# Fewer plain units, more seven-product pairs, and one h matmul moved, in the last stage of a fused retention, soft-MoE and MLP kernel

## The chip, the cores and the metric

The kernel runs on one core of one Trainium2 chip. The metric is device microseconds (us) per execution. The engines are PE (TensorE, with its weight loads as PEld), DVE (VectorE), ACT (ScalarE), POOL (GpSimd) and SP (SyncE, which only issues DMAs here). Each engine works through its own list of instructions in the order written.

## The reference

Three parts follow each other on 3072 tokens (4 batches of 768) of 512 features, all in float32:

```python
# 1 retention: per batch and head, a decayed running state
state = gamma * state + k[t] (x) v[t];  y[t] = scale * q[t] @ state
# 2 soft mixture of experts: 8 experts with 4 slots each
logits = x @ phi                        # 3072 x 32
slot_input = softmax(logits, tokens).T @ x
slot_out = relu(slot_input @ w1[e]) @ w2[e]
x = softmax(logits, slots) @ slot_out
# 3 MLP
h = x @ w_in                            # 3072 x 2048
g = h * sigmoid(1.702 * h)
out = g @ w_out                         # 3072 x 512
```

## The kernel before, in words

The change lies in part 3. There h has a short form: x is a mix of 32 slots, so h = c @ (slot_out @ w_in). The kernel forms G = slot_out @ w_in once (`make_g1`, `make_g2`, tiles `gp`, `rp`, `gst`), and one matmul with 512 columns then gives h of 128 features for 512 tokens. The cost is in g @ w_out.

The tokens stand in six blocks of 512 (block 0 to 5), the 2048 features in sixteen columns f of 128, or eight pairs r of two. To keep float32 precision with a fast matmul type, each operand is split in a high and a low part, and a product is three matmuls (high·high, high·low, low·high). A pair r of one block is done in one of two ways:

- As two plain units. A unit is one h matmul (L641), two ACT activations (L643, L645), the low part on DVE (`lo_unit`, L651, tile `gl`), and twelve matmuls of 512 columns into four banks `acc` (L664): 13 matmuls.
- As one seven-product unit, here called a pair unit. It multiplies 2x2 blocks by a scheme with seven products in place of eight: 7 products x 2 x 3 = 42 matmuls of 256 columns (L727, tiles `P1` to `P7`), and two h matmuls (`s_h`, L693, bank `hb`). For it DVE and ACT build sums of g (`forms`), their high parts `ha`, `hs` (L711) and low parts `la`, `ls`.

`NPL` says how many columns of each block are plain; they come first, in one loop (L1141), block 1 to 5, then the rest of block 0. Its pass u, "step u" from here on, issues h of unit u, the low part of unit u-1, a portion of other work, and the twelve matmuls of unit u-2. The portion is what `work(BUD)` takes from a queue: it runs items until their costs (set by hand, `C1`, `C2` and others) have used up BUD. The queue holds the preparation of the weights: for j = 1, 2, 3 the narrowing of w_in from 64-bit words (`win`, L164 to L168, six DVE instructions for each of two halves), the narrowing of one pair r of w_out (`wfa` or `wfb`, six more), its sums, the G matmuls (`gp`, then `Gh`, `Gl`, then `rp`), and the split of the pair in `bh`, `bl` (L623 on ACT, L688 on DVE). After the loop's units come passes NU and NU+1 (L1146 to L1161), which also prepare the first pair units.

Then all pair units run, block by block (`s_unit`). At the last pair unit of a block, DVE adds the seven products into the block's result; four of these additions (`finish_block`) are put off. The last `NEND` columns of block 5 are plain again (`end_units`): DVE first runs what was put off, then PE's twelve matmuls of each follow, and after the last column DVE adds six pieces to the result (`put`), each sent out by a DMA.

Of the kernel before, what the change touches and what calls it, by code (L numbers as in the profile page):

```python
# [33 lines left out]
NW = 14  # L34
NQ = 3
NX = 5
NPL = (4, 4, 4, 6, 6, 6)
NEND = 4
FULL = (2, 6, 7)
Q = 256  # L40
NWU = 3
# [1 line left out]
KTP = (0, 1, 2, 3, 8, 13, 16, 20)  # L43
KA = (1, 256, 1, 512)
KW = (2, 1, 2)
BUD = 2.3
C1, C2 = 0.34, 0.6
WL = (3, 2)

# [2 lines left out]
def retention_soft_moe_mlp(  # L52
# [575 lines left out]
    def plain_w(f):  # L628
        if f in wh:
            return wh[f], wl[f]  # L630
        return [x[f // 2][:, 2 * (f % 2):2 * (f % 2) + 2].rearrange("p s d -> p (s d)") for x in (bh, bl)]

    units = [(0, f, 0, 1) for f in range(2)]
    units += [(b, f, 0, NPL[b] - 1) for b in range(1, NB) for f in range(NPL[b])]
    units += [(0, f, 2, NPL[0] - 1) for f in range(2, NPL[0])]
    NU = len(units)

    def h_unit(u):
        b, f = units[u][0:2]
        hp = pf.tile([P, 512], F32, tag="h", name=f"h{u}", bufs=3)  # L640
        mm(hp, lhsT=gst[:, f * P:(f + 1) * P], rhs=cT[:, 512 * b:512 * b + 512], start=True, stop=True)  # L641
        gh = fp.tile([P, 512], F32R, tag=("ha", "hs")[u % 2], name=f"gh{u}", bufs=2)
        nc.scalar.activation(out=gh, in_=hp, func=AF.Gelu_apprx_sigmoid)  # L643
        gg = FT[0][:, 2 * (u % 4):2 * (u % 4) + 2].rearrange("p s d -> p (s d)")
        nc.scalar.activation(out=gg, in_=hp, func=AF.Gelu_apprx_sigmoid)  # L645
        gl = fp.tile([P, 512], F32R, tag=("la", "ls")[u % 2], name=f"gl{u}", bufs=2)
        g_hl[u] = (gg, gh, gl)

    def lo_unit(u):
        gg, gh, gl = g_hl[u]  # L650
        nc.vector.tensor_tensor(out=gl, in0=gg, in1=gh.bitcast(F32), op=ALU.subtract)  # L651

    def o_unit(u, t0=0, t1=4, terms=(0, 1, 2)):
        b, f, f0, f1 = units[u]
        _, gh, gl = g_hl[u]
        w0, w1_ = plain_w(f)
        ops = [(gh, w0), (gh, w1_), (gl, w0)]
        if f == f0 and 0 in terms:
            for t in range(t0, t1):
                acc[t] = pf.tile([P, DM], F32, tag="acc", name=f"acc{u}_{t}", bufs=5)  # L660

        def term(t, n):
            g, w = ops[n]
            mm(acc[t], lhsT=g[:, t * P:(t + 1) * P], rhs=w, start=f == f0 and n == 0, stop=f == f1 and n == 2)  # L664

        if u == 0:
            for n in terms:
                for t in range(t0, t1):
                    term(t, n)
        for t in range(t0, t1):  # L670
            if u > 0:
                for n in terms:
                    term(t, n)
            if f == f1 and f0 == 0:
                nc.scalar.copy(out=stage[:, t], in_=acc[t])
                nc.sync.dma_start(out=parts[b][:, t], in_=stage[:, t])
            elif f == f1:
                nc.vector.tensor_tensor(out=pt[0][:, t], in0=acc[t], in1=pt[0][:, t], op=ALU.add)

    span_ = [(NPL[b] // 2, 8 - NEND // 2 * (b == NB - 1)) for b in range(NB)]  # L680
    pairs = [(b, r) for b in range(NB) for r in range(*span_[b])]
# [5 lines left out]
    def vadd(out_, a, b_, op=ALU.add):  # L687
        nc.vector.tensor_tensor(out=out_, in0=a, in1=b_, op=op)  # L688

    def s_h(n, a):  # L690
        b, r = pairs[n]
        f = 2 * r + a
        mm(PB["h"], lhsT=gst[:, f * P:(f + 1) * P], rhs=cT[:, 512 * b:512 * b + 512], start=True, stop=True)  # L693
        t = FT[0]
        nc.scalar.activation(out=t[:, 3 * a:3 * a + 2].rearrange("p s d -> p (s d)"), in_=PB["h"],  # L695
                             func=AF.Gelu_apprx_sigmoid)
        if a == 0:
            vadd(t[:, 2], t[:, 0], t[:, 1], ALU.subtract)

    def s_sum1():  # L700
        t = FT[0]
        vadd(t[:, 5:7], t[:, 0:4:2], t[:, 3:4].to_broadcast([P, 2, Q]))

    def s_sum2():
        t = FT[0]
        vadd(t[:, 7], t[:, 4], t[:, 6], ALU.subtract)

    def s_hi(n, k):
        c0, c1 = FORM[k]
        AH[n, k] = fp.tile([P, c1 - c0, Q], F32R, tag="h" + k, name=f"h{k}_{n}", bufs=2)  # L710
        nc.scalar.copy(out=AH[n, k], in_=FT[0][:, c0:c1])  # L711

    def s_lo(n, k):
        c0, c1 = FORM[k]
        AL[n, k] = fp.tile([P, c1 - c0, Q], F32R, tag="l" + k, name=f"l{k}_{n}", bufs=2)
        vadd(AL[n, k], FT[0][:, c0:c1], AH[n, k].bitcast(F32), ALU.subtract)
# [83 lines left out]
    def end_h(x):  # L800
        f, b = KFF - NEND + x, NB - 1
        mm(PB["h"], lhsT=gst[:, f * P:(f + 1) * P], rhs=cT[:, 512 * b:512 * b + 512], start=True, stop=True)
        gh = fp.tile([P, 512], F32R, tag=("ha", "hs")[x % 2], name=f"egh{x}", bufs=2)
        nc.scalar.activation(out=gh, in_=PB["h"], func=AF.Gelu_apprx_sigmoid)
        gg = FT[0][:, 2 * x:2 * x + 2].rearrange("p s d -> p (s d)")
        nc.scalar.activation(out=gg, in_=PB["h"], func=AF.Gelu_apprx_sigmoid)
        gl = fp.tile([P, 512], F32R, tag=("la", "ls")[x % 2], name=f"egl{x}", bufs=2)
        end_hl[x] = (gg, gh, gl)
# [5 lines left out]
    def end_units():  # L814
# [11 lines left out]

        for x in range(NEND):
            f = KFF - NEND + x
            w0, w1_ = plain_w(f)
            _, gh, gl = end_hl[x]  # L830
            ops = [(gh, w0), (gh, w1_), (gl, w0)]
            last = x == NEND - 1
            if last:
                put(3, slice(0, DM), at_[3], False)
            for t in range(3 if last else 4):
                for i, (g, w) in enumerate(ops):
                    mm(at_[t], lhsT=g[:, t * P:(t + 1) * P], rhs=w, start=x == 0 and i == 0,  # L837
                       stop=i == 2 and (last or (t == 3 and x == NEND - 2)), skip_group_check=True)
                if t == 1 and x + 2 < NEND:
# [11 lines left out]
    with tc.manual_schedule():  # L851
# [241 lines left out]
        def work(budget):  # L1093
            while budget > 0:
                if not queue and not ready:
                    if todo:
                        todo.pop()()
                    elif pend:
                        ready.append(pend.pop(0)[1])
                    else:  # L1100
                        return
                c, fn = (ready or queue).pop(0)
                fn()
                budget -= c
                for p in pend:
                    p[0] -= c
                ready.extend(p[1] for p in pend if p[0] <= 0)
                pend[:] = [p for p in pend if p[0] > 0]
# [32 lines left out]
        for u in range(5, NU + 2):  # L1141
            if u < NU:
                h_unit(u)
                lo_unit(u - 1)
                work(BUD)
            elif u == NU:  # L1146
                lo_unit(u - 1)
                work(1000)
                assert len(raws) == 1 and not (queue or todo or pend or ready), raws
                PB["h"] = pf.tile([P, 512], F32, tag="h", name="hb", bufs=3)  # L1150
                s_h(0, 0)
            else:
                s_h(0, 1)
                s_sum1()
                s_hi(0, "a")
                s_sum2()
                s_lo(0, "a")
                s_hi(0, "s")
                s_lo(0, "s")
                s_h(1, 0)  # L1160
            o_unit(u - 2)  # L1161
        for p, tag in ((2, "acc"), (4, "h"), (1, "h"), (7, "acc"), (5, "acc"), (6, "acc"), (3, "acc")):
            PB[p] = pf.tile([P, 2, Q], F32, tag=tag, name=f"P{p}", bufs=3 if tag == "h" else 5)
        n7 = [x for p_ in zip(pair_narrow(7, 0), pair_narrow(7, 1)) for x in p_]
# [83 lines left out]
```

## Time and profile before

| | |
|---|---|
| median of 3 runs | 453.2 us (453.13 to 453.81) |
| the profiled execution: time, span | 453.41 us, 451.6 us |
| PE, DVE, ACT busy | 97%, 74%, 45% |
| PE clock granted | full speed (2.4 GHz) in all slices |

The span is what the profiler's records cover; 1.8 us of the execution's time lie outside. The retention and expert parts fill the first 160 us, the plain units run from there to 264 us, the pair units to 436 us, the end units and the last DMAs to the end. PE is nearly always busy, so the questions are how much PE work a change removes and whether PE then has to wait.

### The profile page before, as it was taken

Reading aid. Unit: us, or ns where it says so; the run is one execution under the profiler, and the core shown is the slowest. Engines: PE = TensorE matmul, PEld = TensorE weight load, DVE = VectorE, ACT = ScalarE, POOL = GpSimd, SP = SyncE. Lnnn points to the kernel's source line nnn. Section 1 sums busy time; section 2 is a strip of 40 time slices with the busy share of each in tenths; the row PEclk is TensorE's granted clock in tenths of the full one; section 3 lists DMA queues with packets and bytes.
Section 4 is the critical chain, followed back from the end, with each engine's and each line's share of the span. In section 5 each row is a group of like instructions: output and inputs, shape, how many; then the busy total and the mean of one; then the engine's idle time right before and its main releaser. Section 6 shows DMA issues by size and latency. Waiting matters only on the chain.

```text
span 451.6 us, 9953 instructions
## 1 busy us (share of the span) xinstructions
PE 436.6 (97%) x4125; PEld 362.9 (80%) x4125; DVE 332.7 (74%) x594; ACT 205.2 (45%) x351; POOL 48.3 (11%) x53
## 2 busy tenths in 40 slices
PE   8999999899999989999999999999999999999996
PEld 4877877687433467788888889999999999999995
DVE  2455665565455577988979789897797797988984
ACT  1323232323120166563657655655555565565530
POOL 3344343434000000000000000000000000000000
PEclk9999999999999999999999999999999999999999
DMA  8999999998899958588455402001301301311022
GB/s 297 407 401 402 402 371 406 339 405 315 315 394 409 382 211 280 162 304 286 155 218 187 161 26 94 1 1 46 112 30 48 138 4 48 140 46 50 20 75 93
DMA packets 27693, 92.40 MB, mean 205 GB/s; under 512 B 2880, under 2 KB 4320, under 8 KB 23296
## 3 DMA queue, kind: packets, MB, share of 16 engines
q1 hardware_dynamic: 27248, 91.24, 54.8%
q8 instruction: 32, 0.52, 0.5%
q10 hardware_dynamic: 288, 0.36, 0.3%
q0 software_dynamic: 112, 0.16, 0.1%
q14 instruction: 13, 0.11, 0.1%
HBM read 79.17 MB, written 12.58 MB: 203 GB/s over the span
## 4 chain that ended last, share of the span: by engine, by line
PE 83%; DMA 10%; DVE 3%; ACT 1%; issue 1%; POOL 0%; DVEq 0%; SPq 0%; ACTq 0%; POOLq 0%
PE P L727 34%; PE acc L664 18%; DMA qt<-qt_dram 10%; PE sc L212 4%; PE hb L693 4%; PE hp L487 3%; PE y L261 3%; PE eo L512 3%; PE y L257 2%; PE P L837 2%; PE h L641 1%; PE xp L282 1%; PE wu L867 1%; PE op L368 1%; PE tq L530 1%; PE st L269 1%
## 5 line engine op out<-in xcount | busy, mean ns | idle before, releaser
L688 DVE TENSOR_TENSOR forms<-forms 128x256 f32<-128x256 f32 (+1 forms) x93 | 47.5, 511 | 22.4 <-ACT forms L695 21.0
L695 ACT ACTIVATE forms<-hb 128x512 f32<-128x512 f32 x62 | 37.1, 598 | 54.7 <-PE hb L693 34.9
L664 PE MATMUL acc<-wo_hl,gh 128*128 128x512 f32 x192 | 59.8, 394 | 0.4 <-ACT gh L643 0.4
L727 PE MATMUL P<-bh,la 128*128 128x256 f32 x208 | 58.9, 283 | 0.0
L727 PE MATMUL P<-bl,ha 128*128 128x256 f32 x208 | 58.8, 283 | 0.0
L727 PE MATMUL P<-bh,ha 128*128 128x256 f32 x208 | 58.7, 282 | 0.0
L216 DVE TENSOR_TENSOR pt<-sc,ca_t 128x512 f32<-128x512 f32 x44 | 28.3, 685 | 22.9 <-PE sc L212 22.9
L727 PE MATMUL P<-bh,hs 128*128 128x256 f32 x156 | 44.1, 283 | 0.0
L727 PE MATMUL P<-bh,ls 128*128 128x256 f32 x156 | 44.1, 282 | 0.0
L727 PE MATMUL P<-bl,hs 128*128 128x256 f32 x156 | 44.0, 282 | 0.0
L664 PEld LDWEIGHTS acc<-wo_hl,gh 128*128 128x128 f32 x192 | 35.4, 188 | 8.1 <-issue 0.6
L727 PEld LDWEIGHTS P<-bl,ha 128*128 128x128 f32 x208 | 39.4, 189 | 1.1
L727 PEld LDWEIGHTS P<-bh,ha 128*128 128x128 f32 x208 | 39.4, 190 | 0.0
L727 PEld LDWEIGHTS P<-bh,la 128*128 128x128 f32 x208 | 39.4, 189 | 0.0
L688 DVE TENSOR_TENSOR la<-forms,ha 128x1024 fp32r<-128x1024 f32 x31 | 37.9, 1222 | 0.0
L664 PE MATMUL acc<-wo_hl,gl 128*128 128x512 f32 x96 | 37.3, 394 | 0.3 <-DVE gl L651 0.3
L711 ACT CAST ha<-forms 128x1024 fp32r<-128x1024 f32 x31 | 32.6, 1051 | 6.4 <-DVE forms L688 5.6
L643 ACT ACTIVATE gh<-h 128x512 fp32r<-128x512 f32 x30 | 18.0, 600 | 32.7 <-PE h L641 23.9
L711 ACT CAST hs<-forms 128x768 fp32r<-128x768 f32 x31 | 26.0, 838 | 10.1 <-DVE forms L688 7.4
L727 PEld LDWEIGHTS P<-bl,hs 128*128 128x128 f32 x156 | 29.5, 189 | 1.2
L727 PEld LDWEIGHTS P<-bh,hs 128*128 128x128 f32 x156 | 29.5, 189 | 0.0
L727 PEld LDWEIGHTS P<-bh,ls 128*128 128x128 f32 x156 | 29.5, 189 | 0.0
(224 smaller groups left out, 915.3 us busy)
## 6 DMA issues: line engine op xcount, KB each, us to landing
w<-w_dram SPq DMA_DIRECT2D x36, 512.0 KB, 7.7
w<-w_dram SPq DMA_DIRECT2D x14, 1024.0 KB, 8.7
ktv<-ktv_dram SPq DMA_DIRECT2D x20, 512.0 KB, 8.3
wi<-w_in_dram SPq DMA_DIRECT2D x7, 1024.0 KB, 5.6
wo<-w_out_dram SPq DMA_DIRECT2D x7, 1024.0 KB, 4.9
parts<-stage SPq DMA_DIRECT2D x24, 256.0 KB, 3.4
pt<-parts SPq DMA_DIRECT2D x6, 1024.0 KB, 4.8
qt<-qt_dram SPq DMA_DIRECT2D x21, 256.0 KB, 6.4
```

What stands on the lines that cost most here:

```text
L212: mm(sc[hh][:, a, :], lhsT=kT[hh * D:(hh + 1) * D, a, :], rhs=q_[hh * D:(hh + 1) * D, a, :], start=True, stop=True)
L216: nc.vector.tensor_tensor(out=pt[hh], in0=sc[hh], in1=mask[:, None, :].to_broadcast([P, NP, P]), op=ALU.mult)
L261: mm(out_(a, hh ^ (a & 1)), lhsT=vt[:, 2 * a + (hh ^ (a & 1)), :], rhs=pt[hh ^ (a & 1)][:, a, :], start=(c == 0 and a < 2), stop=True, ski ...
L487: mm(hp[32 * j:32 * j + 32, :], lhsT=slotT[:, k, :], rhs=w[:, j, :], start=(k == 0), stop=(k == KDM - 1))
L512: mm(op[32 * j:32 * j + 32, :], lhsT=hT[:, kk, 32 * j:32 * j + 32], rhs=w[:, j, :], start=(kk == 0), stop=(kk == 3))
L643: nc.scalar.activation(out=gh, in_=hp, func=AF.Gelu_apprx_sigmoid)
L664: mm(acc[t], lhsT=g[:, t * P:(t + 1) * P], rhs=w, start=f == f0 and n == 0, stop=f == f1 and n == 2)
L688: nc.vector.tensor_tensor(out=out_, in0=a, in1=b_, op=op)
L693: mm(PB["h"], lhsT=gst[:, f * P:(f + 1) * P], rhs=cT[:, 512 * b:512 * b + 512], start=True, stop=True)
L695: nc.scalar.activation(out=t[:, 3 * a:3 * a + 2].rearrange("p s d -> p (s d)"), in_=PB["h"], func=AF.Gelu_apprx_sigmoid)
L711: nc.scalar.copy(out=AH[n, k], in_=FT[0][:, c0:c1])
L727: mm(PB[p][:, t], lhsT=g[:, c], rhs=w, start=r == span_[b][0] and t == 0 and i == 0, stop=r == span_[b][1] - 1 and i == 2, skip_group_chec ...
```

## The change

```diff
-NPL = (4, 4, 4, 6, 6, 6)
-NEND = 4
+NPL = (4, 4, 4, 4, 6, 6)
+NEND = 2
...
-BUD = 2.3
+BUD = 2.5
...
                 s_lo(0, "a")
                 s_hi(0, "s")
                 s_lo(0, "s")
-                s_h(1, 0)
             o_unit(u - 2)
+        s_h(1, 0)
```

Block 3 has four plain columns in place of six, and block 5 two in place of four at the end. So the loop has 28 units (NU) where it had 30, there are 33 pair units where there were 31, and two end units where there were four. The 25 steps that call `work(BUD)` become 23, and each may take 2.5. The first h of the second pair unit, `s_h(1, 0)`, is issued behind the last plain unit's twelve matmuls, not ahead of them.

In the loop the new budget changes what stands between two low parts on DVE. Of DVE's list, from step 7 on; `gl6` is the low part of unit 6, `win1` and `wfa` are the weights being prepared, `Gl512` is the low part of G that the second group of G matmuls needs. Before:

```order
L651 TENSOR_TENSOR gl6_2461<-forms_2266,gh6_2458 128x512
L168 SCALAR_TENSOR_TENSOR win1_2438<-wi1_1_2363,win1_2438 128x512 x2
L164 TENSOR_SCALAR wfa_2135<-wo2_2436 128x512 x2
L166 SCALAR_TENSOR_TENSOR wfa_2135<-wo2_2436,wfa_2135 128x512
L651 TENSOR_TENSOR gl7_2487<-forms_2266,gh7_2484 128x512
L166 SCALAR_TENSOR_TENSOR wfa_2135<-wo2_2436,wfa_2135 128x512
L168 SCALAR_TENSOR_TENSOR wfa_2135<-wo2_2436,wfa_2135 128x512 x2
L688 TENSOR_TENSOR wfa_2135<-wfa_2135 128x512
L688 TENSOR_TENSOR wfa_2135<-wfa_2135 128x256 x2
L651 TENSOR_TENSOR gl8_2521<-forms_2266,gh8_2518 128x512
L565 TENSOR_TENSOR Gl512_2573<-gp1_2554,Gh512_2571 128x128
```

And now, from step 6 on:

```order
L651 TENSOR_TENSOR gl5_2434<-forms_2266,gh5_2431 128x512
L164 TENSOR_SCALAR win1_2438<-wi1_1_2363 128x512 x2
L166 SCALAR_TENSOR_TENSOR win1_2438<-wi1_1_2363,win1_2438 128x512 x2
L168 SCALAR_TENSOR_TENSOR win1_2438<-wi1_1_2363,win1_2438 128x512 x2
L651 TENSOR_TENSOR gl6_2462<-forms_2266,gh6_2459 128x512
L164 TENSOR_SCALAR wfa_2135<-wo2_2436 128x512 x2
L166 SCALAR_TENSOR_TENSOR wfa_2135<-wo2_2436,wfa_2135 128x512 x2
L168 SCALAR_TENSOR_TENSOR wfa_2135<-wo2_2436,wfa_2135 128x512 x2
L651 TENSOR_TENSOR gl7_2489<-forms_2266,gh7_2486 128x512
L688 TENSOR_TENSOR wfa_2135<-wfa_2135 128x512
L688 TENSOR_TENSOR wfa_2135<-wfa_2135 128x256 x2
L565 TENSOR_TENSOR Gl512_2550<-gp1_2531,Gh512_2548 128x128
```

Six narrowing instructions stand between two low parts where there were five, so `gl7` is the last low part ahead of `Gl512`, where it was `gl8`.

On PE the same shift moves the second group of G matmuls, `rp1`, of which the second needs `Gl512`. `acc6` are the banks of block 2. Before:

```order
L664 MATMUL acc6_3_2534<-wo_hl1_2134,gh8_2518 128x512 x2
L664 MATMUL acc6_3_2534<-wo_hl1_2134,gl8_2521 128x512
L641 MATMUL h11_2610<-cT_2126,gst_2127 128x512
L572 MATMUL rp1_2617<-Gh512_2571,selhl_2128 128x128
L573 MATMUL rp1_2617<-Gl512_2573,selhl_2128 128x128
```

Now:

```order
L664 MATMUL acc6_3_2555<-wo_hl0_2133,gh6_2459 128x512 x2
L664 MATMUL acc6_3_2555<-wo_hl0_2133,gl6_2462 128x512
L641 MATMUL h9_2568<-cT_2126,gst_2127 128x512
L572 MATMUL rp1_2579<-Gh512_2548,selhl_2128 128x128
L573 MATMUL rp1_2579<-Gl512_2550,selhl_2128 128x128
```

`rp1` stands in step 9, one step behind `gp1`, where it stood in step 11, two steps behind `gp1` in step 9. The second and third round of preparation (j = 2, 3) take five steps each, where they took six.

At the program's end DVE's list loses the low parts of the third and fourth end unit (`egl2`, `egl3`); `pt5` is the result of block 5, `wfa` holds sums of products. Before:

```order
L688 TENSOR_TENSOR pt5_4563<-P5_3245,pt5_4563 128x2x256
L688 TENSOR_TENSOR pt5_4563<-P3_3247,pt5_4563 128x2x256
L688 TENSOR_TENSOR pt5_4563<-pt5_4563,wfa_2135 128x2x256 x4
L688 TENSOR_TENSOR egl2_5122<-forms_2266,egh2_5119 128x512
L688 TENSOR_TENSOR egl3_5140<-forms_2266,egh3_5137 128x512
L688 TENSOR_TENSOR pt5_4563<-P7_3244,pt5_4563 128x512
L688 TENSOR_TENSOR pt5_4563<-P2_3241,pt5_4563 128x512
```

Now:

```order
L688 TENSOR_TENSOR pt5_4525<-P5_3207,pt5_4525 128x2x256
L688 TENSOR_TENSOR pt5_4525<-P3_3209,pt5_4525 128x2x256
L688 TENSOR_TENSOR pt5_4525<-pt5_4525,wfa_2135 128x2x256 x4
L688 TENSOR_TENSOR pt5_4525<-P7_3206,pt5_4525 128x512
L688 TENSOR_TENSOR pt5_4525<-P2_3203,pt5_4525 128x512
L688 TENSOR_TENSOR pt5_4525<-P4_3204,pt5_4525 128x512
```

The six closing additions follow directly on the four that were put off.

## Rows read from the trace of the kernel before

**Rows 1.** The page, busy time and share of the span by engine.

```profile
PE 436.6 (97%) x4125; PEld 362.9 (80%) x4125; DVE 332.7 (74%) x594; ACT 205.2 (45%) x351; POOL 48.3 (11%) x53
```

**Rows 2.** Chain that ended last: start, us, what; plain, pair and block-end pieces.

```profile
240.34 2.72 PE acc L664 x12
243.29 2.72 PE acc L664 x12
...
382.04 3.60 PE P L727 x30
387.52 3.60 PE P L727 x30
```

**Rows 3.** DVE's timeline, steps 5 to 10: start, us, instruction, idle before it.

```profile
179.86 0.68 DVE L651 TENSOR_TENSOR gl<-forms,gh 128x512 fp32r<-128x512 f32 x1
180.46 0.76 DVE L164 TENSOR_SCALAR win<-wi 128x512 uint32<-128x512 uint32 x2
181.13 1.29 DVE L166 SCALAR_TENSOR_TENSOR win<-wi,win 128x512 uint32<-128x512 uint32 x2
182.34 0.69 DVE L168 SCALAR_TENSOR_TENSOR win<-wi,win 128x512 uint32<-128x512 uint32 x1
...
191.63 1.61 DVE L688 TENSOR_TENSOR wfa<-wfa 128x512 f32<-128x512 f32 x3
193.16 0.68 DVE L651 TENSOR_TENSOR gl<-forms,gh 128x512 fp32r<-128x512 f32 x1
193.76 0.28 DVE L565 TENSOR_TENSOR Gl<-gp,Gh 128x128 fp32r<-128x128 f32 x1
```

**Rows 4.** PE's timeline, steps 6 to 11.

```profile
179.78 0.39 PE L641 MATMUL h<-cT,gst 128*128 128x512 f32 x1
...
183.04 0.39 PE L641 MATMUL h<-cT,gst 128*128 128x512 f32 x1
...
189.15 0.39 PE L641 MATMUL h<-cT,gst 128*128 128x512 f32 x1
...
193.33 0.39 PE L641 MATMUL h<-cT,gst 128*128 128x512 f32 x1
...
196.32 0.39 PE L641 MATMUL h<-cT,gst 128*128 128x512 f32 x1
...
196.61 0.28 PE L573 MATMUL rp<-Gl,selhl 128*128 128x128 f32 x1
...
200.22 0.39 PE L641 MATMUL h<-cT,gst 128*128 128x512 f32 x1
```

**Rows 5.** Busy time by engine in the loop's steps.

```profile
178.00:258.00 80.00, 80.00 (x443) 64.94 (x442) 70.33 (x125) 49.30 (x92) 0.00 (x0) 1.00 0.63 212
```

**Rows 6.** Timelines in a later round: PE's h, then DVE's split waiting for ACT.

```profile
213.24 0.39 PE L641 MATMUL h<-cT,gst 128*128 128x512 f32 x1
215.29 2.30 DVE L688 TENSOR_TENSOR bl<-wfb,bh 128x512 fp32r<-128x512 f32 x3 [2.56 <-ACT bh L623]
```

**Rows 7.** Timelines from the last plain unit to the fourth pair unit: PE, DVE, PE.

```profile
260.58 0.39 PE L693 MATMUL hb<-cT,gst 128*128 128x512 f32 x1
261.66 0.50 PE L693 MATMUL hb<-cT,gst 128*128 128x512 f32 x1 [0.69 <-ACT forms L695]
...
261.64 1.15 DVE L688 TENSOR_TENSOR forms<-forms 128x512 f32<-128x512 f32 x2 [2.26 <-ACT forms L695]
...
280.09 1.22 DVE L688 TENSOR_TENSOR la<-forms,ha 128x1024 fp32r<-128x1024 f32 x1
...
281.43 0.32 PE L727 MATMUL P<-bh,la 128*128 128x256 f32 x1
```

**Rows 8.** Timelines of the end: PE's first matmul of the end units, then DVE.

```profile
436.03 0.40 PE L837 MATMUL P<-bh,egh 128*128 128x512 f32 x1
...
441.11 1.49 DVE L688 TENSOR_TENSOR egl<-forms,egh 128x512 fp32r<-128x512 f32 x2
444.87 3.39 DVE L688 TENSOR_TENSOR pt<-P,pt 128x512 f32<-128x512 f32 x6 [2.27 <-PE P L837]
```

## The prediction, made before the changed kernel ran

> **What bounds the kernel now.** I read the page first. PE is busy for 97% of the span, DVE for 74% [rows 1], and the granted clock is at its upper level, 2.4 GHz, throughout, so PE's own work is the first suspect. The chain of waits gives its price: a plain unit starts every 2.95 us (243.29 less 240.34), and a pair unit, with its two h matmuls, every 5.48 (387.52 less 382.04) [rows 2]. PE is continuous there. Then I read DVE's and PE's timelines side by side through the loop, where the budget changes. Over 80 us of it DVE is busy for 70.33 [rows 5]; the 9.7 that are left are not spread evenly. From 179.86 until Gl ends at 194.04 DVE has no idle time at all [rows 3]: it runs one list, and PE waits for results far down in it. PE shows this already: step 6 starts at 179.78 and step 7 at 183.04 [rows 4], 3.26 apart, 0.31 more than a plain unit, because the low part that step 6 needs started only at 179.86. Last I read the change to the pair units and the end, where the additions close the chain [rows 7, 8].
>
> **The change part by part.** All sums are made against the profiled execution, 453.41 us, which is 0.2 above the median of the three runs.
>
> *The units.* Four plain units go (4 x 2.95 = 11.80), two pair units come (2 x 5.48 = 10.96) [rows 2]. On PE alone that is -0.84. The number of block ends stays.
>
> *A rule that speaks against it.* The rows give 2.72/12 = 227 ns per matmul of 512 columns and 3.60/30 = 120 ns per one of 256 [rows 2], so halving the columns nearly halves the price. The Trainium skill, TensorE: Matmul & The Clock Gate, section Back-to-back issue gap, gives streams with weight loads 131 ns at 512 columns and 81 at 128, a price that falls far less than the columns; by an estimate of 98 ns at 256 from that page, a pair unit would take 42 x 0.098 + 2 x 0.131 = 4.4 us against 3.4 for two plain units, and this part would be +1.9. By that rule, the trace disagrees (227 and 120 ns), and the trace decides.
>
> *The budget.* DVE's steps in the rows: a low part takes 0.60 to the next start (179.86 to 180.46), a narrowing pair by shift 0.67, a pair by scalar_tensor_tensor 1.21 (181.13 to 182.34) [rows 3]. A step with a low part and six narrowings so takes 0.60 + 0.67 + 1.21 + 1.21 = 3.69 on DVE, against 2.95 on PE. Before, it was five narrowings, 3.08. The changed list has three such steps in a row in each round. Nothing before 179.86 changes on any engine, so I can walk on from there.
>
> Low part 5 starts at 179.86 + 3.69 = 183.55, low part 6 at 187.23, low part 7 at 190.91; the three sums follow it (0.60 + 0.07 for the start, and 1.53 from 191.63 to 193.16 [rows 3]), and Gl runs from 193.11 to 193.39. On PE, step 7 starts at 183.04 as before and waits for low part 5. From step 6 I take that the wait is the low part's start less the step's start plus 0.23 (0.08 there, wait 0.31): 0.74. Step 8 starts at 183.04 + 2.95 + 0.74 = 186.73. It holds gp now, and a step with gp takes 4.18 (189.15 to 193.33) [rows 4], so step 9 starts at 190.91. Its second G matmul, due 0.29 later at 191.20 (196.61 less 196.32 [rows 4]), needs Gl, which ends at 193.39. It waits 2.2. That is 2.95 in the first round; before, steps 7 and 8 together lost 0.22 (189.15 less 183.04 less 2 x 2.945) [rows 4], so it costs 2.7 more. In the kernel before the same matmul came at 196.61, 2.6 after its Gl: two more units had run.
>
> In a later round the split of the pair starts 2.05 after the step's h (213.24 to 215.29), since ACT's casts stand behind that step's activations, and takes 2.22 to the next start [rows 6]; the next low part starts 4.27 after that h, while a step with rp takes 3.90 (196.32 to 200.22) [rows 4]. So DVE enters the next round 0.37 late, and three steps add 0.74 each: 2.59. Gl then ends 2.59 + 2.20 + 0.28 = 5.07 after its step's h, and rp is due 4.18 + 0.29 = 4.47 after it: a wait of 0.6. The second round is spared: the wait of 2.2 in the first lets DVE enter it some 0.8 early. The third pays 0.6. Behind it the last two pairs of weights bring DVE about 2.9 late again at step 24, by the same counting: 0.2 more.
>
> Waits in the loop: 2.7 + 0.6 + 0.2 = +3.5. Its bounds: the first 2.7 rests on a list without gaps and could only be less if those instructions ran shorter, so I keep 2.5 as the low end; the high end is 4.5, if the casts of the fifth pair, which ACT now runs ahead of block 4's four copies, must wait for all of the sums and PE then waits for its banks. I take 3.5. DMAs: each raw load is issued when a buffer is narrowed and is used at least two steps later; SP issues them behind the stores of the same blocks as before, and I cost this at nothing.
>
> *The moved h.* Before, PE issued one h at 260.58 and the next at 261.66, waiting 0.69 for ACT to empty the bank [rows 7]: 1.08 where a matmul of 512 columns takes 0.23, so the move frees 0.85 on PE. What is late next is DVE. From 261.64, when the first sums start, it runs without a gap through three pair units and the narrowing put between them, until the low part that starts at 280.09 and ends at 281.31; PE's matmul that needs it issues at 281.43 and already waits for it (0.32 where its neighbours take 0.28) [rows 7]. That list starts from the same h at 260.58, so at the fourth pair unit the gain is spent. I take 0; the bounds are -0.85 and +0.2, since the additions of the last plain unit now stand ahead of a sum that ACT's cast needs.
>
> *The end.* The first end matmul is at 436.03, and DVE's last six additions end at 444.87 + 3.39 = 448.26, 12.23 later [rows 8]. With two units less, PE would allow 12.23 - 5.89 = 6.34. But DVE must first finish the last pair's additions and the four put off: it is through with them at 441.11, 5.08 after the first end matmul [rows 8], and that list hangs on the last products, not on the end units, whose two 2.95 us covered it. Six additions of 0.60 or less (two are half as long: 3.2 in all) then end at 8.3. So 1.9 of the 5.89 is given back; bounds 1.7 and 2.1, by the row's 3.39.
>
> Sum: -0.84 + 3.5 + 0 + 1.9 = +4.6. The profiled execution would take 458.0, a median 457.8.
>
> **The rivals.**
>
> *PE's count decides.* If DVE's list did not hold PE, -0.84 and -0.85 are gained: 451.7, a median of 451.5. For it: PE is at 97%, DVE at 74% [rows 1], and DVE has 9.7 us to spare in the loop [rows 5]. The place where it would have to show is step 9, and it decides if Gl ends before 191.2. Against it: the list to Gl has no gap, and is counted in single rows. The Trainium skill, Perfetto Trace Analysis, section Identifying the Most-Contended Engine, says to improve the engine with the highest occupancy, and that is PE; by that rule the change is a gain. The trace agrees on occupancy (97%) and disagrees in those 14 us, where DVE is at 100%.
>
> *Only one of the two backlogs shows.* If the end is hidden after all, 457.8 - 1.9 = 455.9; if only the end shows, 453.2 - 0.84 + 1.9 = 454.3. For it: both use the same counting of DVE's starts. Against: they rest on different rows.
>
> *More waits than counted.* ACT's casts ahead of the copies cost PE up to 1.0, and the reordered sums 0.2: 458.0 to 459.0. For it: ACT's list is also strict. Against: ACT has time to spare, 49.30 of 80 us busy [rows 5].
>
> **How the numbers follow.** The forecast has 0.70, with 457.0 to 458.6 as its own range; more waits 0.11; one backlog alone 0.13; PE's count 0.06. The range of 455.2 to 459.2 leaves out the gain, the case of the end alone, and a little above. A measurement of this kernel can tell about 0.2% (0.9 us) from no change. Slower holds the forecast, more waits and nearly all of one backlog: 0.90. The case of 454.3 is at the border and gives most of 0.04 for the same; faster has 0.06.
>
> **What would show it.** Right: PE waiting about 2.2 us at L573, once, for DVE's Gl at L565, and about 0.6 in the third round; step 8 near 186.7; the last plain unit's end only about 2.3 us earlier than before, where the two units would give 5.9; no gap between the two h of the first pair units, and the same DVE start times behind them; DVE's six closing additions following the four without idle time. Wrong: PE without waits at L573, or DVE idle ahead of the closing additions. A time under 454 would say that DVE's list did not hold PE; one over 459.2 that ACT or a DMA does too.

## The result and the profile after

The changed kernel took 459.03 us (median of four runs, 458.25 to 459.43), the kernel before 453.19 beside it: a ratio of 1.0138, 95% interval 1.0111 to 1.0165, or 6.3 us more (5.0 to 7.5). The forecast was 457.8. The median lies just inside the forecast range; the ratio, taken on the 453.2 us of before, puts the time at 459.4, just above it. The profiled execution took 459.34 us, of which the span is 457.6, 6.0 more than before.

The page of after, busy time, the granted clock in 40 slices, and the shares of the chain that ended last:

```profile
PE 438.5 (96%) x4161; PEld 365.5 (80%) x4161; DVE 337.3 (74%) x600; ACT 207.0 (45%) x351; POOL 48.4 (11%) x53
...
PEclk9999999999999999989999999999999999999999
...
PE 72%; DVE 14%; DMA 6%; issue 3%; ACT 2%; POOL 1%; DVEq 0%; SPq 0%; ACTq 0%; POOLq 0%
```

The occupancies are those of before [rows 1]; nothing in them shows the loss. The 8 in the clock's row does: it stands in the loop's first round of weight preparation.

DVE's timeline there (start, us, instruction), the answer to [rows 3]:

```profile
182.91 0.69 DVE L651 TENSOR_TENSOR gl<-forms,gh 128x512 fp32r<-128x512 f32 x1
...
190.28 0.69 DVE L651 TENSOR_TENSOR gl<-forms,gh 128x512 fp32r<-128x512 f32 x1
190.88 1.61 DVE L688 TENSOR_TENSOR wfa<-wfa 128x512 f32<-128x512 f32 x3
192.41 0.28 DVE L565 TENSOR_TENSOR Gl<-gp,Gh 128x128 fp32r<-128x128 f32 x1
```

Low parts 5 and 7 start 7.37 apart, two steps of 3.69. This execution reached step 6 at 179.15, 0.63 sooner than before's; the forecast's times less 0.63 are 182.92, 190.28 and 192.48. PE's timeline, answering to [rows 4], with the idle time before an instruction and what ended it:

```profile
182.37 0.39 PE L641 MATMUL h<-cT,gst 128*128 128x512 f32 x1
183.65 0.50 PE L664 MATMUL acc<-wo_hl,gl 128*128 128x512 f32 x1 [0.45 <-DVE gl L651]
186.09 0.40 PE L641 MATMUL h<-cT,gst 128*128 128x512 f32 x1
190.29 0.39 PE L641 MATMUL h<-cT,gst 128*128 128x512 f32 x1
192.75 0.33 PE L573 MATMUL rp<-Gl,selhl 128*128 128x128 f32 x1 [2.01 <-DVE Gl L565]
...
197.99 0.39 PE L641 MATMUL h<-cT,gst 128*128 128x512 f32 x1
...
228.78 0.33 PE L573 MATMUL rp<-Gl,selhl 128*128 128x128 f32 x1 [0.41 <-DVE Gl L565]
```

Step 7 takes 3.72, 0.77 more than a plain step; the wait for Gl holds the second G matmul from 190.58 to 192.75, 2.17; the third round's is 0.41 in the row (its step takes 4.48 in place of 3.90). All of these were forecast. What was not: step 9 to step 10 is 7.70, where the wait explains 3.90 + 2.17 = 6.07. The same stretch cut in five, with the length, busy time and instructions of PE, PEld, DVE, ACT and POOL, then the granted clock, the DMA share and GB/s:

```profile
187.43:190.29 2.86, 2.86 (x17) 2.36 (x13) 2.86 (x7) 0.59 (x2) 0.00 (x0) 1.00 0.88 215
190.29:192.75 2.46, 0.45 (x4) 0.19 (x2) 2.39 (x7) 2.04 (x4) 0.00 (x0) 1.00 0.93 310
192.75:193.58 0.83, 0.83 (x7) 0.83 (x8) 0.83 (x2) 0.83 (x1) 0.00 (x0) 1.00 1.07 331
193.58:197.99 4.41, 4.41 (x15) 3.44 (x14) 4.41 (x8) 0.69 (x2) 0.00 (x0) 0.61 0.87 343
197.99:200.93 2.94, 2.94 (x14) 2.44 (x13) 2.65 (x7) 1.09 (x2) 0.00 (x0) 1.00 0.33 67
...
194.00:196.00 2.00, 2.00 (x7) 1.51 (x6) 2.00 (x3) 0.37 (x1) 0.00 (x0) 0.50 1.09 423
```

PE works without a gap from 193.58 to 197.99, but at a mean granted clock of 0.61; the last row, a cut inside that stretch, has 0.50, the lower level of 1.2 GHz. It follows on 2 us of standing still. Its twelve matmuls take 4.41 us; at the full clock the same twelve take 2.82 (e3, below).

The move of h, PE's two h matmuls and DVE's low part that ends the gain, answering to [rows 7]:

```profile
259.12 0.39 PE L693 MATMUL hb<-cT,gst 128*128 128x512 f32 x1
262.07 0.39 PE L693 MATMUL hb<-cT,gst 128*128 128x512 f32 x1
...
278.81 1.22 DVE L688 TENSOR_TENSOR la<-forms,ha 128x1024 fp32r<-128x1024 f32 x1
```

PE no longer waits between the two h (the last plain unit's matmuls fill that time), but from the first of them to that low part it is 19.69 where it was 19.51. The end, PE's first closing matmul and DVE, answering to [rows 8]:

```profile
445.82 0.64 PE L837 MATMUL P<-wo_hl,egh 128*128 128x512 f32 x2
...
445.37 2.02 DVE L688 TENSOR_TENSOR wfa<-P,wfa 128x512 f32<-128x512 f32 x3 [1.06 <-PE P L727]
447.30 1.28 DVE L688 TENSOR_TENSOR pt<-P,pt 128x512 f32<-128x512 f32 x2
448.50 2.49 DVE L688 TENSOR_TENSOR pt<-pt,wfa 128x512 f32<-128x512 f32 x4
450.90 3.14 DVE L688 TENSOR_TENSOR pt<-P,pt 128x512 f32<-128x512 f32 x6
```

DVE has no idle time from 445.37 to 454.04, 8.22 behind the first closing matmul; before, the six additions waited 2.27 for PE.

### The profile page after: what moved, and what is told of

The parts are those of the page before. It is cut to its first block, busy times and chain, and to the rows that moved or that the text cites. A ratio compares the mean times of both kernels' runs of the same rounds, so it can differ in the third digit from the quotient of the medians.

```text
span 457.6 us, 10039 instructions
## 1 busy us (share of the span) xinstructions
PE 438.5 (96%) x4161; PEld 365.5 (80%) x4161; DVE 337.3 (74%) x600; ACT 207.0 (45%) x351; POOL 48.4 (11%) x53
## 4 chain that ended last, share of the span: by engine, by line
PE 72%; DVE 14%; DMA 6%; issue 3%; ACT 2%; POOL 1%; DVEq 0%; SPq 0%; ACTq 0%; POOLq 0%
PE P L727 33%; PE acc L664 10%; DMA qt<-qt_dram 6%; PE sc L212 4%; PE hb L693 3%; PE hp L487 3%; PE y L261 3%; PE eo L512 3%; PE y L257 2%; PE xp L282 2%; DVE gl L651 1%; DVE wfa L688 1%; DVE win L166 1%; PE wu L867 1%; PE op L368 1%
## 5 line engine op out<-in xcount | busy, mean ns | idle before, releaser
L688 DVE TENSOR_TENSOR forms<-forms 128x256 f32<-128x256 f32 (+1 forms) x99 | 50.7, 512 | 24.3 <-ACT forms L695 22.7
L727 PE MATMUL P<-bh,la 128*128 128x256 f32 x224 | 63.8, 285 | 0.1
L727 PE MATMUL P<-bl,ha 128*128 128x256 f32 x224 | 63.3, 283 | 0.0
L727 PE MATMUL P<-bh,ha 128*128 128x256 f32 x224 | 63.3, 282 | 0.0
L727 PE MATMUL P<-bh,hs 128*128 128x256 f32 x168 | 47.5, 283 | 0.0
L727 PE MATMUL P<-bh,ls 128*128 128x256 f32 x168 | 47.4, 282 | 0.0
L727 PE MATMUL P<-bl,hs 128*128 128x256 f32 x168 | 47.4, 282 | 0.0
L727 PEld LDWEIGHTS P<-bl,ha 128*128 128x128 f32 x224 | 42.4, 189 | 1.2
L727 PEld LDWEIGHTS P<-bh,la 128*128 128x128 f32 x224 | 42.4, 189 | 0.6 <-DVE la L688 0.5
L727 PEld LDWEIGHTS P<-bh,ha 128*128 128x128 f32 x224 | 42.4, 189 | 0.0
```

The source lines that it names most:

```text
L727: mm(PB[p][:, t], lhsT=g[:, c], rhs=w, start=r == span_[b][0] and t == 0 and i == 0, stop=r == span_[b][1] - 1 and i == 2, skip_group_chec ...
```

## The experiments

In these later runs the times of one kernel lie some 5 us apart, and the traces reach step 6 anywhere from 176.7 to 183.4, ahead of all that was edited. So each trace is read by three stretches that leave this out: A from h of step 6 to the first h of the first pair unit, B from there to the first closing matmul, C from there to the span's end. The sum is against before. The last column is the ratio of times, with its interval; "fall" says whether the granted clock fell from 1.00 to 0.50 for a few us behind the first round's wait for Gl. Stretches and clock are those of one traced execution of each kernel.

| kernel | A | B | C | sum | fall | ratio |
|---|---|---|---|---|---|---|
| before | 77.85 | 178.40 | 15.57 | | no | |
| after | 77.02 | 189.65 | 11.78 | +6.63 | yes | 1.0138 (1.0111 to 1.0165) |
| e1 budget 2.3 | 72.04 | 190.53 | 11.75 | +2.50 | no | 1.0081 (1.0048 to 1.0114) |
| e2 before, budget 2.5 | 83.80 | 178.46 | 15.61 | +6.05 | yes | 1.0116 (1.0080 to 1.0152) |
| e3 wait filled | 75.42 | 189.65 | 11.74 | +4.99 | no | 1.0126 (1.0088 to 1.0164) |
| e4 four on GpSimd | 75.45 | 189.65 | 11.46 | +4.74 | no | 1.0168 (1.0138 to 1.0199) |
| e5 after again | 75.41 | 189.55 | 11.69 | +4.83 | no | 1.0143 (1.0106 to 1.0181) |
| e6 rp a step later | 73.49 | 189.83 | 11.76 | +3.26 | no | 1.0072 (1.0049 to 1.0096) |
| e7 two on GpSimd | 77.00 | 189.56 | 10.67 | +5.41 | yes | 1.0125 (1.0092 to 1.0159) |
| e8 h back | 77.00 | 189.37 | 11.74 | +6.29 | yes | 1.0123 (1.0076 to 1.0171) |
| e9 before, two at the end | 77.82 | 183.89 | 11.73 | +1.62 | no | 1.0022 (0.9994 to 1.0050) |
| e10 before, block 3 | 71.98 | 184.77 | 15.61 | +0.54 | no | 0.9997 (0.9973 to 1.0022) |
| e11 rest undone | 72.04 | 190.26 | 10.69 | +1.17 | no | 1.0014 (0.9986 to 1.0043) |
| e12 wait half filled | 75.47 | 189.55 | 11.79 | +4.99 | no | one run |
| e13 before, rp early | 91.73 | 178.35 | 15.61 | +13.87 | three | 1.0275 (1.0178 to 1.0373) |
| e14 after, third trace | 77.07 | 189.52 | 11.77 | +6.54 | yes | one run |
| e15 filled, again | 75.43 | 189.62 | 11.79 | +5.02 | no | one run |

**e1, the budget undone.**

```diff
-BUD = 2.5
+BUD = 2.3
```

> The changed kernel with the budget of a step back at 2.3. Theory (DVE's list, made too long for a step by the budget, holds PE; all of the loop's loss is that): from step 6 to h of the first pair unit PE took 77.02 us in the changed kernel and 77.85 before, with two plain units of 2.95 less, so 77.02 - (77.85 - 5.90) = 5.07 us were waits and what followed from them. They go: 459.0 - 5.1 = 453.9 us, no wait of 2 us for Gl, and no fall of the granted clock near step 9. Rival 1 (two units less leave DVE no room, whatever the budget): the list's last 2.4 us (the low part of the fifth pair) now stand in the last step and hold the first pair unit: up to 456.4. Rival 2 (the budget only moves the wait elsewhere): 459.0.

A is 72.04, 4.98 less than after: the loop's loss is the budget's. The sum fell by 4.1 only, since B grew by 0.88. The time fell less still (1.0081 is 3.7 us over before, the sum +2.5); that rest is in none of the three stretches of its trace. ACT's list shows why B grew, at the last plain unit, with the PE matmul that waits:

```profile
252.06 1.05 ACT L623 CAST bh<-wfa 128x1024 fp32r<-128x1024 f32 x1 [0.43 <-DVE wfa L688]
253.02 2.04 ACT L675 COPY stage<-acc 128x512 f32<-128x512 f32 x4
...
253.64 0.73 PE L664 MATMUL acc<-wo_hl,gh 128*128 128x512 f32 x2 [0.45 <-ACT stage L675]
```

With two steps fewer the last pair's cast stands ahead of the copies that free PE's banks. So the larger budget had bought some 0.9 at the loop's end, for 5.0 in its rounds.

**e2, the budget alone.**

```diff
-BUD = 2.3
+BUD = 2.5
```

> The kernel before with only the budget raised to 2.5. Theory: the steps up to 17 are then the same instructions as in the changed kernel, so the same waits and the same fall of the clock: +5.1 us, 458.3 (457.5 to 458.5). Rival 1 (waits come from having fewer units to hide the work behind; the budget alone is free with 38 units): 453.2 to 453.6. Rival 2 (the budget costs its waits, but the slow matmuls after them have another cause that the fewer units brought): 453.2 + 3.4 = 456.6.

The kernel before (30 units in its loop and four at the end, not the 38 of the expectation) shows, with that one number, the same row at L573, 2.01 us for Gl, the same fall (step 9 to 10 takes 7.68), and +5.95 in A, 1.06 of it in a later step where PE waits for ACT's copies (0.77 in the row). The budget alone costs nearly as much as the whole change, and the waits come without fewer units.

**e3, e12 and e15, the wait filled.**

```diff
         gh, gl = G_t.pop(f0)
+        for _ in range(9 if f0 == 512 else 0):
+            mm(rp, lhsT=cT[:, 0:P], rhs=cT[:, 0:512], start=True, stop=True)
```

This is the edit of e3 and of e15; e12 has 4 in place of 9.

> The changed kernel with nine idle matmuls of 512 columns put ahead of the first round's rp matmuls, into the same tile that rp then overwrites: nine of 227 ns are 2.04 us, the length of the wait for Gl. Theory (PE standing still is what took the granted clock to its lower level): the wait for Gl shrinks to under 0.2 us, the granted clock stays at 1.00 and the 12 matmuls behind rp take 2.7 to 2.8 us and not 4.40: 459.0 - 1.7 = 457.3. Rival 1 (the slow matmuls belong to the transfers that land at the same time, 423 GB/s, or to DVE's and ACT's casts): they stay at 4.4 us, 459.0. Rival 2 (the fall comes from the load that the engines make together, and more matmuls make it worse or put it later): 459 to 460.

In e3 PE's stretches up to the first G matmul with Gl, the other G matmuls, and the twelve matmuls behind them read:

```profile
189.09:191.38 2.29, 2.27 (x12) 1.69 (x10) 2.22 (x6) 2.09 (x4) 0.00 (x0) 1.00 0.96 349
191.38:192.21 0.83, 0.83 (x7) 0.83 (x8) 0.83 (x2) 0.83 (x1) 0.00 (x0) 1.00 1.00 274
192.21:195.03 2.82, 2.82 (x15) 2.31 (x14) 2.82 (x4) 0.64 (x2) 0.00 (x0) 1.00 1.06 412
```

PE reaches the same matmul as late as before, but busy, and then runs at the full clock: 2.82, not 4.41. DMA moves as much (412 GB/s) and DVE is as busy, so rival 1 of the expectation, transfers or casts, is out for this trace. One trace is little, though, because e4 and e5 (below) have the full wait and no fall. Nor does the time show it: 1.0126 can't be told from the 1.0143 of the changed kernel run again (e5).

> The changed kernel with four idle matmuls of 512 columns ahead of the first round's rp, so that PE stands for some 1.1 us and not for 2.0. Traces with the full wait showed the granted clock at 0.50 behind it in four of six. Theory (the length of the standing still matters): no fall, step 9 to 10 takes 6.1 us. Rival (any wait there sets it off, or it has nothing to do with the wait): 7.7.

The wait was 1.10 us, and no fall came.

> The changed kernel with nine idle matmuls in the wait once more, for a second trace. Theory (PE that doesn't stand still keeps its clock): step 9 to 10 takes 6.1 to 6.2 us and the granted clock is 1.00 in the whole loop. Rival (chance): 7.7 in two of three.

Again 2.0 us of busy waiting and step 9 to 10 in 6.08, at 1.00 in the whole loop.

**e4 and e7, the end.** e4 puts all four put-off additions of the last block on GpSimd, e7 two of them:

```diff
+        if b == NB - 1:
+            for i, j, k, eng in ((0, 0, 0, nc.gpsimd), (1, 0, 2, nc.gpsimd), (0, 1, 3, None), (1, 1, 2, None)):
+                vadd(quad(b, i, j), quad(b, i, j), e[:, k], eng=eng)
+            return
```

This list is e7's; e4 has `nc.gpsimd` in all four. The lines that give `vadd` its `eng` are left out here.

> The changed kernel with the four put-off additions of the last block on GpSimd in place of DVE. Theory (DVE's closing additions set the end: gapless from the end of the pair unit, DVE ended 2.6 us after PE): four additions of some 0.6 us leave DVE's list, and the end comes back to PE's last matmul plus one addition: 459.0 - 2.1 = 456.9 (GpSimd's 128x512 additions took 1.04 us each earlier in this kernel, 4.2 us beside 5.5 us of matmuls). Rival 1 (the last store's DMA, not DVE, sets the end): 459.0. Rival 2 (GpSimd's additions come too late for the closing ones, or slow DVE's): 458 to 460.

C shrank by 0.3 only. GpSimd took 1.27 to 1.65 us for each, and its last two, which need DVE's sums, held DVE's closing additions for 1.41 and 0.56 us: the end hung on GpSimd instead.

> The changed kernel with two of the four put-off additions of the last block on GpSimd, those whose operands are ready first (quads 0,0 and 1,0). With all four there, DVE's end came only 0.25 us sooner (7.97 us behind the first closing matmul against 8.22), since GpSimd took 1.3 us for each, one behind the other. Theory (DVE's list is what the end hangs on): two additions of 0.62 us leave it, none of GpSimd's is late, so DVE's end comes at 8.22 - 1.2 = 7.0 us behind the first closing matmul. Rival 1 (GpSimd's slow additions hold the closing ones here too): 7.9 to 8.2. Rival 2 (both slow each other down): over 8.2.

DVE's last rows in e7, and GpSimd's two:

```profile
445.18 2.01 DVE L688 TENSOR_TENSOR wfa<-P,wfa 128x512 f32<-128x512 f32 x3 [1.05 <-PE P L727]
447.11 1.28 DVE L688 TENSOR_TENSOR pt<-P,pt 128x512 f32<-128x512 f32 x2
448.42 1.29 DVE L688 TENSOR_TENSOR pt<-pt,wfa 128x512 f32<-128x512 f32 x2
449.63 3.14 DVE L688 TENSOR_TENSOR pt<-P,pt 128x512 f32<-128x512 f32 x6
...
443.62 1.65 POOL L688 TENSOR_TENSOR pt<-pt,wfa 128x512 f32<-128x512 f32 x1 [300.07 <-ACT wfa L772]
446.68 1.29 POOL L688 TENSOR_TENSOR pt<-pt,wfa 128x512 f32<-128x512 f32 x1 [1.40 <-DVE wfa L688]
```

DVE ends 7.14 behind the first closing matmul, expected 7.0, and C is 1.1 less: DVE's list sets the end. The Trainium skill, GPSIMD Engine Reference, section Engine selection, calls GPSIMD about half as fast as the vector engine for additions of two inputs; the traces agree, with 1.29 and 1.65 us for one on GpSimd, against 0.62 on DVE (2.49 for four, in after's rows above).

**e5 and e14, the changed kernel again.**

> The changed kernel once more, unchanged, as the measure for the other runs on the same chip. Of the traces so far that hold the wait of 2.01 us, two (the changed kernel, and before with the budget of 2.5) show the granted clock at 0.50 for some 3.3 us right behind it and one (the run with GpSimd's additions) does not, its step 9 to 10 taking 6.13 us in place of 7.70. Theory: the wait is there again with 2.0 us, and the fall behind it is likely but not certain; 1.3 to 1.4% over before. If the fall is bound to the wait, step 9 to 10 takes 7.7 again; if it is chance, some 6.1.

PE's h of step 9, the wait, and h of step 10:

```profile
191.35 0.39 PE L641 MATMUL h<-cT,gst 128*128 128x512 f32 x1
...
193.84 0.33 PE L573 MATMUL rp<-Gl,selhl 128*128 128x128 f32 x1 [2.04 <-DVE Gl L565]
...
197.47 0.39 PE L641 MATMUL h<-cT,gst 128*128 128x512 f32 x1
```

The wait is there with 2.04 us, the fall is not: step 9 to 10 takes 6.12, and A is 75.41, 2.44 less than before, where the forecast's terms give -5.90 + 3.5 = -2.4.

> The changed kernel, unchanged, for one more trace of the wait of 2.0 us. Four of six traces with that wait show the fall right behind it, none of eight without it (or with 1.1 us) shows one in the loop. Theory: step 9 to 10 takes 7.7 us, with about two chances in three; 6.1 without the fall. Nothing in between.

7.74, with the fall. So the wait is always the same (2.01 to 2.06 us in the row), and the fall came behind it in five of seven traces (after, e2, e7, e8, e14; not e4 and e5).

**e6, the rp matmuls asked for later.**

```diff
-                queue.append((0.6, lambda: make_g2(...)))
+                late_ = lambda: make_g2(...)
+                queue.append((0.6, lambda: pend.append([1.1, (0, late_)])))
```

> The changed kernel with the rp matmuls of each round put one step later (DVE's and ACT's lists stay but for one cast; only PE's order changes). Theory (PE stands for Gl because rp is asked for too early, and everything behind the wait follows from it): from step 6 to h of the first pair unit 77.0 us become 77.0 - 2.2 - 0.5 - 1.6 = 72.7, the wait of 0.45 us for a low part at step 7 stays; 459.0 - 4.3 = 454.7. Rival 1 (DVE's list as a whole is the bound; PE only meets it elsewhere): the waits come back as waits for low parts or gp and the stretch takes 75 us, 457. Rival 2 (the clock falls whatever the wait): 74.3 us, 456.3.

PE's steps 9 and 10 now:

```profile
189.53 0.39 PE L641 MATMUL h<-cT,gst 128*128 128x512 f32 x1
192.74 0.39 PE L641 MATMUL h<-cT,gst 128*128 128x512 f32 x1
192.97 0.22 PE L572 MATMUL rp<-Gh,selhl 128*128 128x128 f32 x1
193.03 0.28 PE L573 MATMUL rp<-Gl,selhl 128*128 128x128 f32 x1
```

No wait, no fall. A is 73.49, 3.5 less than after (1.9 less than e5, which had no fall), with no instruction taken from any engine. It missed 72.7 by 0.8: near the loop's end a low part is late by 0.40 in the row (its step takes 3.67). Part of rival 1 is therefore true, since DVE's list still holds PE there, but in the rounds the waits for Gl came from the place of the rp matmuls.

**e8, h moved back.**

```diff
                 s_lo(0, "s")
+                s_h(1, 0)
             o_unit(u - 2)
-        s_h(1, 0)
```

> The changed kernel with h of the second pair unit back ahead of the last plain unit. Theory (the moved matmul changes which of two waits PE has, ahead of the first pair unit's la, and saves nothing): the stretch from h of the first pair unit to the first closing matmul takes 189.65 us with the move; without it 189.4 to 189.7 (the wait of 0.69 us for ACT's forms comes back and 0.9 us of later waiting goes). Rival (the move saved its wait, as it is meant to): 190.3 to 190.5. In the total both are within what the measurement can tell, so the stretch decides.

B is 189.37 without the move and 189.52 to 189.65 with it (e5, e14, after): the move loses some 0.2 and saves nothing. At the budget of 2.3 it is much the same: 190.53 with it (e1), 190.26 without (e11).

**e9 and e10, the two unit counts alone.**

```diff
-NEND = 4
+NEND = 2
```

> The kernel before with only the closing plain units cut from four to two (one more pair unit in the last block). Theory (the end is not PE's but DVE's then): 5.48 us for the pair unit, and from the first closing matmul to the span's end 11.8 us in place of 15.57, as in the changed kernel, so +5.48 - 3.79 = +1.7 us, 454.9; the loop's stretch stays at 77.85. Rival (PE's count decides there too: 5.48 for twice 2.95): -0.4, 452.8.

C falls by 3.84 where two units are worth 5.9, B grows by 5.49, and DVE's last six additions follow the four without idle time: +1.62, by stretches. The ratio alone, 1.0022, would not tell it from no change.

```diff
-NPL = (4, 4, 4, 6, 6, 6)
+NPL = (4, 4, 4, 4, 6, 6)
```

> The kernel before with only the fourth block cut from six to four plain units, budget still 2.3. Theory: the loop's stretch is that of the changed kernel with the budget of 2.3, 72.0 us (5.8 less), the pair unit adds 5.48, and the fifth pair's casts stand in ACT's list ahead of the copies of the last plain unit that PE waits for (0.77 us of waiting in that run): 77.85 to 72.04 and 178.40 to 184.7, +0.4, 453.6. Rival 1 (PE's count, nothing comes in between): -0.4, 452.8. Rival 2 (DVE's list, two steps short, holds the first pair unit): up to 456.

+0.54 by stretches, with ACT's 0.77 in B's first step. In time no difference can be told.

**e11, fewer units with the rest undone or mended.** Budget 2.3, h back, two additions on GpSimd as in e7.

> The changed kernel with its fewer plain units kept and the rest undone or mended: budget 2.3, h of the second pair unit back ahead of the last plain unit, two of the last block's four put-off additions on GpSimd. Theory: of the 5.1 to 6.6 us by which the stretches of the changed kernel are longer, the budget's waits and the clock (4.1 net of ACT's wait of 0.8), 1.05 at the end and 0.25 for h go: about +1.2 us over before, 454.4, so the fewer plain units do not pay even then. Rival (the parts hide one another and only one shows): +2.5 as with the budget alone, 455.7. Rival 2 (once nothing waits, PE's count shows): -0.8, 452.4.

+1.17 by stretches, so the parts add up. (The traced execution was 458.81 us, 5 above this kernel's median; what it lost lies ahead of step 6.) The ratio, 1.0014, is no change that can be told. No version beat the kernel before.

**e13, the wait in the kernel before.**

```diff
-                queue.append((2.5, lambda: make_g1(...)))
-                queue.append((0.6, lambda: make_g2(...)))
+                queue.append((2.5, lambda: (make_g1(...), make_g2(...))))
+                queue.append((0.6, lambda: None))
```

> The kernel before, budget 2.3, with each round's rp matmuls put right behind its gp matmuls, so that PE stands still for Gl there without any of the changed kernel's edits; DVE's list stays. In the first round gp ends at 190.55 in the trace of before and Gl at 194.04, so PE waits 3.0 to 3.5 us; in the other two rounds, with PE later by as much, some 0.5 to 1.6 us. Theory (PE standing still for about 2 us or more is what the fall of the granted clock comes behind, whatever else is changed): a stretch of 0.50 of some 3.3 us right behind the first round's wait, worth 1.6 us beside the wait's length; nothing behind the two short waits. Rival (the fall needs the fewer plain units or the budget, or lands there by chance): granted clock 1.00 throughout the stretch.

The waits are 2.82, 2.02 and 1.64 us, each with 0.39 us of waiting for Gh ahead of it. With that the first is as long as expected (3.2); the other two are longer than their 0.5 to 1.6. PE's rows at the waits, then for each the stretch of the wait and the one up to the next h:

```profile
195.73 0.33 PE L573 MATMUL rp<-Gl,selhl 128*128 128x128 f32 x1 [2.82 <-DVE Gl L565]
...
219.84 0.33 PE L573 MATMUL rp<-Gl,selhl 128*128 128x128 f32 x1 [2.02 <-DVE Gl L565]
...
243.60 0.33 PE L573 MATMUL rp<-Gl,selhl 128*128 128x128 f32 x1 [1.64 <-DVE Gl L565]
```

```profile
192.70:195.73 3.03, 0.22 (x1) 0.07 (x1) 2.93 (x7) 0.00 (x0) 0.00 (x0) 1.00 0.93 301
195.73:200.97 5.24, 5.24 (x19) 4.40 (x20) 0.55 (x1) 0.59 (x1) 0.00 (x0) 0.67 0.91 334
217.60:219.84 2.24, 0.22 (x1) 0.08 (x1) 2.17 (x6) 0.00 (x0) 0.00 (x0) 1.00 0.83 205
219.84:225.11 5.27, 5.26 (x20) 4.46 (x21) 0.55 (x1) 0.59 (x1) 0.00 (x0) 0.68 0.34 145
241.70:243.60 1.90, 0.26 (x1) 0.12 (x2) 1.83 (x6) 0.00 (x0) 0.00 (x0) 1.00 0.84 207
243.60:248.84 5.24, 5.24 (x20) 4.46 (x20) 0.54 (x1) 0.59 (x1) 0.00 (x0) 0.67 0.30 125
```

All three waits have the fall behind them (the clock is 0.50 from 196.6 to 199.4, for instance), where none was expected behind the last two. The kernel has neither the fewer units nor the budget, DMA moves 125 to 334 GB/s, and DVE is busy for only some 0.55 of each 5.2 us. The rival is out, and so are transfers and DVE's casts as the cause of the slow matmuls. Each wait costs its length and some 1.8 us more: the first step takes 10.16, where gp and rp alone make it 4.18 + 0.95 = 5.13, and 5.0 more is 3.2 of waiting and 1.8 of clock.

## Why the prediction was right and wrong

**The step that failed is the price of the first round's wait in "The budget".** "It waits 2.2" was right, but the wait was priced at its length; the sum has no term for the clock, which in the trace of before kept its upper level through all of PE's work, and the high end of 4.5 allowed for ACT's casts only. PE lost its upper clock behind it and paid 1.6 us again on the twelve matmuls that follow. The loop's waits, forecast at 3.5 with a high end of 4.5, came to 77.02 - (77.85 - 5.90) = 5.1 in the profiled execution. In the trace without the fall (e5) they are 75.41 - 71.95 = 3.5. That the wait brings the fall is shown three ways: five of seven traces with it and all three waits of e13 have it, no trace of the loop without it has it, and PE kept busy or asked later keeps its clock. Why two of the seven escaped is open. The times don't show the clock's share by itself: only one of the four measured executions has a trace, and e5's traced one, without this fall, still took 458.82 us, 1.1 of it because it reached step 6 that much later.

The traces show the same ahead of step 6, where PE waits for loads. Two such rows, from e11 and e6:

```profile
73.70 1.16 PE L212 MATMUL sc<-qt,ktv 64*128 64x128 f32 x16 [2.65 <-DMA qt<-qt_dram]
...
89.18 1.05 PE L212 MATMUL sc<-qt,ktv 64*128 64x128 f32 x14 [1.68 <-DMA qt<-qt_dram]
```

Behind the first the clock falls to 0.50 (0.54 is the mean from 74.5 to 78.0), behind the second it stays at 1.00. Of the waits for loads in all kept traces, the five of 1.73 to 2.65 us (e4 twice, e5, e11, e13) have a fall behind them, and none of those up to 1.68 us has. One more fall, in e1 near 162, follows no wait over 0.7 us; it stays unexplained.

**Right:** the place and length of the waits (step 7: 0.74 forecast, 0.77 measured; Gl: 2.2 and 2.17; third round: 0.6 and 0.58; end of the loop: 0.2 and 0.19), the spared second round, and the cause, a DVE list without gaps. e2 shows that the budget alone suffices, e6 that the place of rp decides.

**The units:** 4 x 2.95 against 2 x 5.48 holds: e9's B grew by 5.49, and A fell by 5.87 in e10. The gain of 0.84 is there and is nowhere seen in a time.

**The moved h:** 0 was taken, the stretches say a loss of about 0.2, the upper bound. The rival of -0.85 is refuted by e8.

**The end:** the additions were forecast to end at 8.3 and end at 8.22. C gives back 5.90 - 3.79 = 2.1 of two units, against 1.9 taken and a bound of 2.1. e7 shows the cause.

**The rivals:** PE's count does not decide, and both backlogs show. "More waits than counted" came nearest in time for another reason than the one it named: in after, ACT's casts cost PE nothing. They did in e1, e2 and e10, 0.8 to 1.1.

The sum by its terms: -0.84 for the units, 5.1 for the waits with their clock, 0.2 for h, 2.1 for the end, 6.6; the execution's earlier start took 0.6 off the span.

## What to carry to other kernels

A budget per step must be summed as durations on the engine that runs it: 3.69 us of DVE against 2.95 of PE made three full steps into one wait of 2 us, while DVE stood at 74%. When two engines run in step, ask for a late result later before making the list shorter; moving each round's rp matmuls by a step gave back 3.5 us, 1.6 of it the clock's. And price a wait on TensorE of about two microseconds at its length plus what its clock may take, here 1.6 us.

## What the runs showed of the hardware that was not expected

Behind a standing still of 2.0 us TensorE's granted clock fell from 1.00 to 0.50, that is from 2.4 to 1.2 GHz, in five of seven traces, and behind three of three waits in e13 (1.64 us at the shortest, 0.39 behind another). Ahead of step 6 it fell behind five of five waits for loads of 1.73 to 2.65 us. In all of these traces it still reads 1.00 up to the end of the wait, and the fall begins with PE at work again, at once (e4's first) or as late as 1.9 us behind the wait (e8). In after, the stretch of 0.83 us right behind the wait reads 1.00 and the next has 0.61. PE then works through it without a gap, and an occupancy of 96% does not show it; the twelve matmuls' 4.41 us does. Behind waits of 0.4 and, in one trace, 1.10 us in the loop, and of up to 1.68 us for loads ahead of it, none was seen; the one fall near 162 in e1 is left over.
